# Attention and two MLPs on one core: the second pair's transposes and 46 unread products placed in front of the first scores, and a few tiles moved in on-chip memory

## The chip, the cores and the metric

The kernel runs on one core of one Trainium2 chip. The metric is device microseconds of one execution, smaller is better. The core has the engines TensorE (PE, with its weight loads shown as PEld), VectorE (DVE), ScalarE (ACT), GpSimd (POOL), and SyncE (SP), which here only issues DMAs.

## What is computed

Attention over 4 batches and 8 heads, 576 positions, head size 64, with a causal mask and a gate bias made from running sums of `max(s, 0)`; its output goes through a first MLP (512 to 1024 to 512, a softmax-weighted unit with a layer norm) and a second (512 to 2048 to 512). Cut to what matters:

```python
scores = scale * np.matmul(q, k.transpose(0, 1, 3, 2))
cum = np.cumsum(np.maximum(s, 0.0), axis=-1)
bias = -(cum[:, :, :, None] - cum[:, :, None, :])
scores = np.where(causal, -1000000000.0, scores + np.minimum(bias, 0.0))
attn = softmax(scores)
x = (attn @ v) as [2304, 512]
h = x @ w_in;  e = exp(h - max(h));  solu = h * e / (sum(e) + 1e-09)
x = layer_norm(solu) * g_ln @ w_out
h = x @ w2_in;  out = (h * np.clip(h + 3.0, 0.0, 6.0) / 6.0) @ w2_out
```

## The kernel before

Heads are worked in pairs (two heads of 64 rows side by side on 128 partitions). For a pair `p` of batch 0, `load_qk` (L396) loads q and k in natural order; `prep_whole` (L431 on) **turns** them: TensorE transposes six pieces of q and six of k against the identity matrix `ident` (L441), ACT scales q and DVE copies k out of PSUM (L446, L448). The bias is added by a second product: `gate_rows` makes running sums on DVE (L279 to L283), stores them as rows in DRAM (`rows_d`, L287), and `load_gates` (L428) brings four rows per head into the tiles `whole0` and `whole1`. `qk_whole` (L584) then makes the scores of a query tile `t` (128, 128, 128, 96, 96 rows): per head one product with the gate rows and one with q and k, in the same PSUM bank. Tiles 0 and 1 of all four pairs of batch 0 go first, later tiles afterwards. `tops` (L532, DVE) adds the mask and takes the row maxima, `exps` (L544, ACT) the exponentials, `norm_part` the reciprocals of the sums (L640, L641, DVE) and the scaling (L645, POOL); `tr` (L679) transposes the result, `av` (L708) multiplies by v.

The first MLP: `ffn1_x` splits a token tile in a high and a low part (`xh` on DVE L795, `xl` on POOL L799); `ffn1_h` (L813) is three products per piece with `w_in_h` and `w_in_l`; `ffn1_z` (L879) transposes, and `ffn1_out` (L900) multiplies `zh`, `zl` by `w_out_h`, `w_out_l`. The second MLP is L1072 and L1103. The weights come as 64-bit words and are decoded on ACT, DVE and POOL during the attention of batch 0.

The order of the work is not the order of the source. `Plan.add` records each step with its engine, an assumed duration, what it reads, writes and holds, and an assumed `lag` until a transfer has landed; `Plan.emit` runs a list scheduler over these numbers and writes every engine's instructions in the order that comes out. The numbers set the order alone: on the chip each instruction waits for the semaphores of what it truly needs. DMAs share eight semaphores in turn, so an issue also waits until the DMA that stands eight places ahead of it has landed.

Tiles are placed in the order in which the program asks for them. A tile pool on the right grows downward: `w_in_h`, `w_in_l`, `w_out` (chunks 0 to 4 of its 8), `g_sb`, then the working tiles `x`, `xh`, `xl`, `st`, `e`, `zh`, `zl`. Counted modulo 512 bytes, the tiles of the second MLP start at 480; in the first MLP `w_in_h` and `w_in_l` start at 448 and `xh`, `xl` at 320; `zh` and `zl` start at 448, `w_out` at 448 for chunks 0 to 4 and at 480 for chunks 5 to 7 (those lie in tiles of their own).

Of the kernel before, what the change touches and what calls it, by code (L numbers as in the profile page):

```python
# [10 lines left out]
F32 = mybir.dt.float32  # L11
# [29 lines left out]
CHUNKS = (3, 3, 4, 4, 4)  # L41
LAG = 2
DELAY = 3.5
X2_AT = 8
HOP_TO_PE, HOP_FROM_PE, HOP = 0.26, 0.2, 0.13

# [142 lines left out]
def kernel(ctx, tc, q, k, v, s, w_in, w_out, g_ln, w2_in, w2_out, out):  # L189
# [50 lines left out]
    def w_out_at(x, c):  # L240
        late = c >= KFF - LATE_OUT
        return w_out_t[x, late][:, c - (KFF - LATE_OUT) * late, :]

    w_out_part(False)
    g_sb = w1p.tile([P, KFF], F32, name="g_sb")


    at = ExitStack()
# [6 lines left out]
        return banks[plan.bank[key]]  # L255


    mask = ap1.tile([P, 480 + P], F32, name="mask")
    nc.gpsimd.memset(mask, 0.0)
    nc.gpsimd.affine_select(out=mask[:, 480:], in_=mask[:, 480:], pattern=[[-1, P]], compare_op=ALU.is_ge, fill=NEG, base=0, channel_multiplier=1)  # L260
# [5 lines left out]
    def gate_rows():  # L266


        s_sb = ap2.tile([P, S], F32, tag="y4", name="s_sb")[:NH]
        one = ap2.tile([P, S], F32, tag="y4", name="one")[:NH]  # L270
        cum = ap2.tile([P, NQ, 2, D], F32, tag="V", name="cum").rearrange("p c j d -> p (c j d)")[:NH, :S]
        pos = ap2.tile([P, PT_COLS], F32, tag="pt", name="pos", bufs=PT).bitcast(F32R)[:NH, : 2 * S]
        neg = ap2.tile([P, PT_COLS], F32, tag="pt", name="neg", bufs=PT).bitcast(F32R)[:NH, : 2 * S]

        def load():
            nc.sync.dma_start(out=s_sb, in_=s.rearrange("b h s -> (b h) s"))

        def sums():
            nc.vector.tensor_scalar_max(s_sb, s_sb, 0.0)  # L279
            nc.vector.tensor_tensor_scan(cum, one, s_sb, 0.0, ALU.mult, ALU.add)  # L280
            nc.vector.tensor_copy(pos[:, :S], cum)
            nc.vector.tensor_sub(pos[:, S:], cum, pos[:, :S].bitcast(F32))
            nc.vector.tensor_scalar_mul(neg, pos.bitcast(F32), -1.0)  # L283

        def put(i, r, src):
            dst = rows_d[:, i, r::2, :]
            nc.sync.dma_start(out=dst, in_=src)  # L287

        def zeros(j):
            whole_t[j] = ap1.tile([P, 4, S], F32, tag=f"stack{j}", name=f"whole{j}")  # L290
            nc.gpsimd.memset(whole_t[j][:, 2:4, :], 0.0)

        plan.add("SP", 0.45, load, writes=["s"], lag=2.0)
        plan.add("POOL", 2.2, lambda: nc.gpsimd.memset(one, 1.0), writes=["one"])
        plan.add("DVE", 3.0, sums, reads=["s", "one"], writes=["c"])
        ones = one.unsqueeze(1).to_broadcast([NH, 2, S])
        both = lambda c: c.bitcast(F32).rearrange("p (i s) -> p i s", i=2)
        for i, r, src, key in ((1, 0, both(pos), "c"), (0, 1, both(neg), "c"), (0, 0, ones, "one"), (1, 1, ones, "one")):
            plan.add("SP", 0.55, lambda i=i, r=r, src=src: put(i, r, src), reads=[key], writes=[f"rows/{i}{r}"], lag=2.0)
        for j in range(2):  # L300
            plan.add("POOL", 1.3, lambda j=j: zeros(j), writes=[f"zeros{j}"], new=[(f"stack{j}", 1, f"whole{j}")])

# [121 lines left out]
    def load_gates(p, a):  # L424
# [4 lines left out]

        plan.add("SP", 0.8, gates, reads=ROWS_D + [f"zeros{p % 2}", f"whole{p % 2}"], writes=[f"G{p}{a}"], new=[("G", 2, f"G{p}{a}")], lag=2.0)  # L430

    def prep_whole(p, name):

        n = S // 6
        i, raw_key, hl_key = "qk".index(name), f"raw{name}{p}", f"HL{p}"

        def turn(c0, key):
            if name == "q" and c0 == 0:
                hls[hl_key] = ap2.tile([P, 2, S], F32R, tag="HL", name=hl_key).bitcast(F32) if p < 2 else whole_t[p % 2][:, :2, :]
            for c in range(c0, c0 + 3):  # L440
                nc.tensor.transpose(bank(key)[:, (c - c0) * n : (c - c0 + 1) * n], raws[p, name][:n, c, :, :], ident[:n, :n])  # L441

        def put(c0, key):
            to = hls[hl_key][:, i, c0 * n : (c0 + 3) * n]
            if name == "q":
                nc.scalar.mul(to, bank(key)[:, : 3 * n], QK_SCALE)  # L446
            else:
                nc.vector.tensor_copy(to, bank(key)[:, : 3 * n])  # L448

        if name == "q":  # L450
            load_gates(p, 0)
        ring = [("HL0", 2, hl_key)] if p < 2 else []
        home = [] if p < 2 else [f"zeros{p % 2}", f"whole{p % 2}"]
        for c0 in (0, 3):
            key = f"pp{p}{name}{c0}"
            plan.add("PE", 3 * 0.083, lambda c0=c0, key=key: turn(c0, key), reads=[raw_key, *home], writes=[key],
                     new=ring if name == "q" and c0 == 0 else [], bank=key, after=[] if name == "q" and c0 == 0 else [f"pp{p}q0"])
            plan.add(*(("ACT", act(3 * n)) if name == "q" else ("DVE", dve(3 * n))), lambda c0=c0, key=key: put(c0, key), reads=[key, *home], writes=[f"{hl_key}/{name}{c0}"])
# [95 lines left out]
    def qk_whole(p, t):  # L554

        n, w = SZ[t], ST[t] + SZ[t]
        heads = (2 * p, 2 * p + 1)
        late = ST[t] >= CUT
        ts = [i for i in range(NQ) if (ST[i] >= CUT) == late]

        def homes():
            for h, x in zip(heads, "hl"):
                if p % 2 == 0:
                    ys[h, t] = ap2.tile([P, w], F32, tag=f"y{t}", name=f"y{h}_{t}")
                elif t == ts[0]:
                    cols = sum(ST[i] + SZ[i] for i in ts)
                    if late:
                        y = w1p.tile([P, LATE_OUT, DM], F32, tag=f"w_out_{x}1", name=f"yl{h}").rearrange("p c n -> p (c n)")
                    else:
                        y = ap2.tile([P, cols], F32, tag="y2", name=f"yf{h}")  # L570
                    o = 0
                    for i in ts:
                        ys[h, i] = y[:, o : o + ST[i] + SZ[i]]
                        o += ST[i] + SZ[i]

        def mm(c0, c1, keys):
            if c0 == 0:
                homes()
            for m in range(2):
                for j in range(2):  # L580
                    r = slice(j * D, (j + 1) * D)
                    g, hl = gates_at(p, j), hls[f"HL{p}"][r]
                    a, b = (hl[:, 0, :], hl[:, 1, :]) if m else (g[:, 0, :], g[:, 1, :])
                    nc.tensor.matmul(bank(keys[j])[:n, : c1 - c0], lhsT=a[:, ST[t] : w], rhs=b[:, c0:c1], start=(m == 0), stop=(m == 1))  # L584

        pieces = pieces_of(t)
        for c0, c1, at in pieces:
            keys = [f"sc{h}_{t}_{c0}" for h in heads]
            new = []
            if c0 == 0 and p % 2 == 0:  # L590
                new = [(f"y{t}", 2, f"y{h}_{t}") for h in heads]
            elif c0 == 0 and t == ts[0]:
                new = [("wlate", 1, f"yl{p}")] if late else [("y2", 2, f"yf{h}") for h in heads]
            plan.add("PE", 4 * max(0.07, 0.00033 * (c1 - c0)), lambda c0=c0, c1=c1, keys=keys: mm(c0, c1, keys),
                     reads=[f"HL{p}/{x}{c}" for x in "qk" for c in ((0, 3) if late else (0,))] + [f"G{p}{late:d}", f"whole{p % 2}"], writes=keys, new=new, bank=keys, after=[f"sc{heads[0]}_{t}_0"] if c0 else [])
            for h, key in zip(heads, keys):
                plan.add("DVE", dve(c1 - c0), lambda h=h, c0=c0, c1=c1, at=at, key=key: tops(h, t, c0, c1, at, key), reads=[key],
                         writes=[f"{y_key(h, t)}/{c0}", f"nmax{h}_{at}"])
        for h in heads:
            exps(h, t, pieces)  # L600
# [146 lines left out]
    def pairs(a):  # L747
# [3 lines left out]
        for p in range(NPAIR):  # L751
# [2 lines left out]
            turns = [] if last is None else [(0.4, lambda h=h, gi=gi: tr(h, gi)) for gi in ((1, 2, 3) if last[1] else (0,)) for h in (2 * last[0], 2 * last[0] + 1)]  # L754
            extra = []
            if not a:
                if p + 1 < NPAIR:
                    extra = [(0.3, lambda p=p: prep_qk(p + 1, "q")), (0.3, lambda p=p: prep_qk(p + 1, "k"))]
                extra += [(0.0, lambda p=p: load_qk(p + 2))] if p + 2 <= NPAIR else []
                extra += [(0.0, lambda p=p: load_v(p + 1, 0))] if p + 1 < NPAIR else [(0.0, lambda: load_v(0)), (0.0, lambda: load_gates(0, 1))]  # L760
# [44 lines left out]
    def ffn1_h(i, f, kk):  # L805
        key = f"h{i}_{f}"

        def mm():
            if f == kk == 0:
                sts[i] = bcp.tile([P, 16], F32, tag="st", name=f"st{i}")  # L810
                es[i] = bcp.tile([P, 2, 512], F32, tag="e", name=f"e{i}")
            for m in range(3):
                nc.tensor.matmul(bank(key), lhsT=xs[i][m // 2][:, kk, :], rhs=(w_in_l if m == 1 else w_in_h)[:, kk, f * 512 : (f + 1) * 512],  # L813
                                 start=(kk == 0 and m == 0), stop=(kk == KDM - 1 and m == 2))
# [161 lines left out]
    for name in "qk":  # L976
        prep_qk(0, name)
    load_qk(1)
    load_v(0, 0)
    plan.add("SP", 0.5, lambda: nc.sync.dma_start(out=g_sb, in_=g_ln.rearrange("(c p) -> p c", p=P)), writes=["g"], lag=2.0, after=["HL0/k0"])  # L980
    for b, share in enumerate(SHARES):
# [212 lines left out]
```

## Time and profile before

| | us |
|---|---|
| median of 3 runs | 842.57 (842.36 to 842.8) |
| profiled execution, its own time | 840.6 |
| its span | 838.8 |
| PE busy | 810.9 (97%) |
| DVE busy | 438.5 (52%) |
| ACT busy | 399.4 (48%) |
| POOL busy | 209.9 (25%) |

The span runs from the first to the last instruction of the profiled execution; 1.8 us of its time lie outside. A busy PE is an engine with a matmul in flight, whatever its clock. The column PEclk of a table by stretches gives the TensorE clock that was granted, 1.00 being 2.4 GHz and 0.50 being 1.2 GHz. The chain of waits is followed back from the last instruction: each step is what released the next one.

### The profile page before, as it was taken

What the parts mean: (1) busy time and instruction counts of PE and PEld (TensorE: products, weight loads), DVE (VectorE), ACT (ScalarE), POOL (GpSimd) and SP (SyncE); (2) the same over time, 40 slices, a digit from 0 to 9 for tenths busy, and PEclk for the clock granted to TensorE, in tenths of its full rate; (3) what the DMA queues carried; (4) which work ended last, traced back from release to release, by engine and by line L of the source; (5) the groups of instructions that cost most, each with busy time, mean ns of one, the idle gap of its engine ahead of it and who ended that gap; (6) DMA issues with size and microseconds to landing.
All of it is one profiled execution on the core that took longest, in us unless ns stands there. A gap on an engine that the chain in (4) does not pass through costs nothing.

```text
span 838.8 us, 13546 instructions
## 1 busy us (share of the span) xinstructions
PE 810.9 (97%) x4864; PEld 686.1 (82%) x4864; DVE 438.5 (52%) x1125; ACT 399.4 (48%) x928; POOL 209.9 (25%) x309
## 2 busy tenths in 40 slices
PE   3889999999999999999999999999999999999997
PEld 2555688898898889888999999998888888888886
DVE  3787887746855674739826992233222232222221
ACT  2575767755765575736635762244222322232222
POOL 2564644424632364327412220000000000000000
PEclk9999999999999999999999999999999999999999
DMA  6753596855656465323615640012000300010001
GB/s 163 194 150 112 126 214 148 175 121 125 130 119 137 99 130 121 65 95 117 198 38 192 215 152 1 0 63 89 1 0 1 101 1 0 1 51 1 0 1 50
DMA packets 95938, 77.52 MB, mean 92 GB/s; under 512 B 64288, under 2 KB 78112, under 8 KB 95872
## 3 DMA queue, kind: packets, MB, share of 16 engines
q1 hardware_dynamic: 93568, 68.27, 32.7%
q10 hardware_dynamic: 2304, 8.39, 3.0%
q8 instruction: 38, 0.62, 0.3%
q14 instruction: 28, 0.23, 0.1%
HBM read 45.38 MB, written 10.03 MB: 66 GB/s over the span
## 4 chain that ended last, share of the span: by engine, by line
PE 91%; DVE 4%; POOL 2%; DMA 2%; issue 1%; ACT 1%; POOLq 0%; DVEq 0%; SPq 0%; ACTq 0%
PE bank L1072 24%; PE bank L1103 23%; PE bank L900 11%; PE bank L813 10%; PE bank L708 6%; PE bank L679 5%; PE bank L611 5%; PE bank L584 3%; PE bank L879 2%; PE bank L474 1%; POOL y L645 1%; DVE y L532 1%; DMA stack<-HL12k 1%; DMA rows_d<-neg 1%; POOL y L627 0%
## 5 line engine op out<-in xcount | busy, mean ns | idle before, releaser
L1072 PE MATMUL bank<-x2h,w 128*128 128x512 f32 (+1 forms) x640 | 183.7, 368 | 0.0
L1103 PE MATMUL bank<-w,gh 128*128 128x512 f32 x576 | 177.0, 390 | 0.0
L1080 DVE SCALAR_TENSOR_TENSOR g<-g,bank 128x512 f32<-128x512 f32 (+1 forms) x80 | 50.7, 633 | 204.4 <-ACT g L1076 204.1
L1072 PEld LDWEIGHTS bank<-x2h,w 128*128 128x128 f32 x640 | 118.8, 188 | 17.5
L1076 ACT ACTIVATE g<-bank 128x512 f32<-128x512 f32 (+1 forms) x80 | 44.5, 556 | 178.2 <-PE bank L1072 177.9
L1103 PEld LDWEIGHTS bank<-w,gh 128*128 128x128 f32 x576 | 107.7, 188 | 21.0
L1072 PE MATMUL bank<-x2l,w 128*128 128x512 f32 (+1 forms) x320 | 117.8, 368 | 0.0
L1103 PE MATMUL bank<-w,gl 128*128 128x512 f32 x288 | 111.8, 391 | 0.0
L532 DVE CUSTOM_DVE_ANT_0 y<-bank,mask 96x288 f32<-96x288 f32 (+4 forms) x168 | 74.7, 467 | 57.4 <-PE bank L611 38.0
L544 ACT ACTIVATE y<-y,nmax 128x256 f32<-128x256 f32 (+4 forms) x140 | 83.4, 598 | 39.8 <-DVE nmax L532 27.5
L627 POOL TENSOR_SCALAR y<-y,rsum 128x128 f32<-128x128 f32 (+4 forms) x120 | 68.6, 590 | 103.8 <-DVE rsum L623 45.2
L900 PE MATMUL bank<-zh,w_out_h 128*128 128x256 f32 x288 | 82.8, 287 | 0.0
L900 PE MATMUL bank<-zl,w_out_h 128*128 128x256 f32 x288 | 81.2, 282 | 0.0
L900 PE MATMUL bank<-zh,w_out_l 128*128 128x256 f32 x288 | 81.2, 282 | 0.0
L1088 DVE TENSOR_TENSOR gl<-g,gh 128x512 fp32r<-128x512 f32 (+1 forms) x80 | 51.8, 647 | 42.2 <-ACT gh L1084 41.9
L1084 ACT CAST gh<-g 128x512 fp32r<-128x512 f32 (+1 forms) x80 | 46.2, 578 | 47.4 <-DVE g L1080 47.3
L1072 PEld LDWEIGHTS bank<-x2l,w 128*128 128x128 f32 x320 | 60.1, 188 | 7.5
L1103 PEld LDWEIGHTS bank<-w,gl 128*128 128x128 f32 x288 | 54.0, 188 | 11.3
L813 PE MATMUL bank<-w_in_h,xh 128*128 128x512 f32 x144 | 60.9, 423 | 0.8 <-DVE xh L795 0.8
L611 PE MATMUL bank<-stack 128*96 128x288 f32 (+4 forms) x288 | 57.8, 317 | 0.8 <-DMA stack<-HL12k 0.8
L813 PE MATMUL bank<-w_in_h,xl 128*128 128x512 f32 x144 | 56.9, 395 | 0.6 <-POOL xl L799 0.6
L813 PE MATMUL bank<-w_in_l,xh 128*128 128x512 f32 x144 | 56.8, 394 | 0.0
(220 smaller groups left out, 1356.4 us busy)
## 6 DMA issues: line engine op xcount, KB each, us to landing
raw_w2i<-in_moe_w_in_dram SPq DMA_DIRECT2D x16, 512.0 KB
raw_w2o<-in_moe_w_out_dram SPq DMA_DIRECT2D x16, 512.0 KB
rawq<-in_q_dram SPq DMA_DIRECT2D x32, 144.0 KB
rawk<-in_k_dram SPq DMA_DIRECT2D x32, 144.0 KB
x_d<-x2s SPq DMA_DIRECT2D x36, 128.0 KB
out_dram<-ob SPq DMA_DIRECT2D x18, 256.0 KB
raw_wi<-in_moe_w_in_dram ACTq DMA_DIRECT2D x8, 512.0 KB
raw_wo<-in_moe_w_out_dram ACTq DMA_DIRECT2D x8, 512.0 KB
```

What stands on the lines that cost most here:

```text
L532: nc.vector.tensor_tensor_reduce(out=ys[h, t][:n, c0:c1], in0=bank(key)[:n, : c1 - c0], in1=mask[:n, 480 + n - w + c0 : 480 + n - w + c1], ...
L544: nc.scalar.activation(out=y[:n], in_=y[:n], func=AF.Exp, bias=nmax[:n, h, t : t + 1], scale=-1.0, accum_out=sums[:n, h, t : t + 1])
L611: nc.tensor.matmul(bank(key)[:n, : c1 - c0], lhsT=ss[:, 2 - 2 * m, ST[t] : w], rhs=ss[:, 3 - 2 * m, c0:c1], start=(m == 0), stop=(m == 1))
L627: nc.gpsimd.tensor_scalar(ys[h, t][:n], ys[h, t][:n], rsum[:n, h, t : t + 1], 1.0, ALU.mult, ALU.mult)
L708: nc.tensor.matmul(bank(key)[j * D : (j + 1) * D, lo - c0 : c1 - c0], lhsT=vs[v_key(p, a)][:n, jj, j, :], rhs=pts[pt_key(2 * p + j, a)][:n ...
L813: nc.tensor.matmul(bank(key), lhsT=xs[i][m // 2][:, kk, :], rhs=(w_in_l if m == 1 else w_in_h)[:, kk, f * 512 : (f + 1) * 512], start=(kk ...
L900: nc.tensor.matmul(bank(key)[:, : 2 * P], lhsT=w_out_at(w, kk)[:, m * P : (m + 1) * P], rhs=z[:, kk, :], start=(kk == 0 and i == 0), stop= ...
L1072: nc.tensor.matmul(bank(key)[:, :w], lhsT=wt[:, a, 0, c * P : (c + 1) * P], rhs=x[:, c, :w], start=(c == 0 and i == 0), stop=(c == KDM - 1 ...
L1080: nc.vector.scalar_tensor_tensor(out=gg, in0=gg, scalar=6.0, in1=bank(key)[:, :w], op0=ALU.min, op1=ALU.mult)
L1084: nc.scalar.copy(gh[:, :w], gg[:, :w])
L1088: nc.vector.tensor_sub(gl[:, :w], gg[:, :w], gh[:, :w].bitcast(F32))
L1103: nc.tensor.matmul(bank(key), lhsT=g_t[ci, m][1 + i // 2][:, t * P : (t + 1) * P], rhs=w2[m][:, i % 2, 1, :], start=(m == 0 and i == 0), s ...
```

## The change

Four edits. In `pairs` and in the main body the turns of pair 1 are no longer spread over the first steps but planned right after pair 0's, and the first scores of pair 0 must wait until pair 1's last turn has begun (`after=["pp1k3"]`); the gate rows' stores are planned with a lag of 4.5 in place of 2.0. A new helper `keep_clock` issues bf16 products of `ident` with itself (128x256) into the bank that the next step overwrites; nothing reads them: 26 ahead of pair 1's q turn, 10 ahead of its k turn, 10 ahead of the first scores. `g_sb` is placed ahead of `w_out` and `st` grows from 16 to 64 numbers (two buffers), so `xh` and `xl` now start at 448 modulo 512 as `w_in` does, and `w_out` starts at 480 for all eight chunks while `zh`, `zl` stay at 448. A tile of 32 numbers, `apart_too`, moves all attention tiles by 128 bytes; `ident` stays.

```diff
+FILL = dict(q=26, k=10, s=10)
...
+    g_sb = w1p.tile([P, KFF], F32, name="g_sb")
     w_out_part(False)
-    g_sb = w1p.tile([P, KFF], F32, name="g_sb")
...
+    ap1.tile([P, 32], F32, name="apart_too")
     mask = ap1.tile([P, 480 + P], F32, name="mask")
...
-            plan.add("SP", 0.55, lambda i=i, r=r, src=src: put(i, r, src), reads=[key], writes=[f"rows/{i}{r}"], lag=2.0)
+            plan.add("SP", 0.55, lambda i=i, r=r, src=src: put(i, r, src), reads=[key], writes=[f"rows/{i}{r}"], lag=4.5)
...
+    def keep_clock(n, key):
+
+        x = ident.bitcast(BF16)
+        for _ in range(n):
+            nc.tensor.matmul(bank(key)[:, : 2 * P], lhsT=x[:, :P], rhs=x, start=True, stop=True)
...
+            if p == 1 and c0 == 0:
+                keep_clock(FILL[name], key)
...
+            if p == t == c0 == 0:
+                keep_clock(FILL["s"], keys[0])
...
-... after=[f"sc{heads[0]}_{t}_0"] if c0 else [])
+... after=[f"sc{heads[0]}_{t}_0"] if c0 else ["pp1k3"] if p == 0 and not late else [])
...
-                if p + 1 < NPAIR:
+                if 0 < p < NPAIR - 1:
                     extra = [(0.3, lambda p=p: prep_qk(p + 1, "q")), (0.3, lambda p=p: prep_qk(p + 1, "k"))]
...
-                sts[i] = bcp.tile([P, 16], F32, tag="st", name=f"st{i}")
+                sts[i] = bcp.tile([P, 64], F32, tag="st", name=f"st{i}")
...
     load_qk(1)
+    for name in "qk":
+        prep_qk(1, name)
     load_v(0, 0)
```

The start of TensorE's order, before: the turns of pair 0 (`rawq_120`, `rawk_123`), then scores of pair 0 (`whole_126` holds its gate rows) mixed with the turns of pair 1 (`rawq_148`, `rawk_163`).

```order
L441 MATMUL bank_100<-ident,rawk_123 128x96 x3
L584 MATMUL bank_101<-whole_126 128x128
L584 MATMUL bank_102<-HL_138 128x128
L441 MATMUL bank_103<-ident,rawq_148 128x96 x3
L584 MATMUL bank_97<-whole_126 128x256
L584 MATMUL bank_98<-HL_138 128x256
L441 MATMUL bank_99<-ident,rawk_163 128x96 x3
L584 MATMUL bank_103<-whole_135 128x128
L584 MATMUL bank_102<-HL_183 128x256
L441 MATMUL bank_99<-ident,rawq_198 128x96 x3
L679 MATMUL bank_97<-ident,y_0_177 128x128
```

The same place now (L438 is the unread product, L451 the turn, L596 the score, L691 the transpose of `y`; pair 1 is `rawq_149`, `rawk_164`, pair 2 `rawq_229`, `rawk_257`; 26, 10 and 10 pairs of L438 rows stand at the three places).

```order
L451 MATMUL bank_100<-ident,rawk_124 128x96 x3
L438 LDWEIGHTS ident
L438 MATMUL bank_101<-ident 128x256
L451 MATMUL bank_101<-ident,rawq_149 128x96 x3
L451 MATMUL bank_103<-ident,rawk_164 128x96 x3
L596 MATMUL bank_97<-whole_127 128x128
L596 MATMUL bank_100<-HL_139 128x256
L596 MATMUL bank_101<-whole_136 128x128
L596 MATMUL bank_104<-HL_178 128x256
L451 MATMUL bank_97<-ident,rawq_229 128x96 x3
L451 MATMUL bank_100<-ident,rawk_257 128x96 x3
L691 MATMUL bank_101<-ident,y_0_241 128x128
```

Both turns of pair 1 have moved ahead of all scores, the scores of pairs 0 and 1 stand in one block, and pair 2's k turn has moved ahead of the first transposes of `y`.

SP's order at the gate rows, before and now (`whole_126`/`whole_127` for pair 0, `whole_135`/`whole_136` for pair 1; `V0a` is v of pair 0, and the issue shown brings 128x2x64 numbers, 64 KB).

```order
L396 DMA rawk_163<-in_k_dram 96x6x64 [waits DMAHW6_49]
L428 DMA whole_126<-rows_d 4x2x576 [waits DMAHW2_49,DMAHW7_49,DMAHW1_49,Pool_49]
L414 DMA V0a<-in_v_dram 128x2x64
L980 DMA g_sb<-in_moe_g_ln_dram 128x8x1
L428 DMA whole_135<-rows_d 4x2x576 [waits DMAHW3_49,Pool_49]
```

```order
L398 DMA rawk_164<-in_k_dram 96x6x64 [waits DMAHW6_49]
L416 DMA V0a<-in_v_dram 128x2x64 [waits DMAHW7_49]
L994 DMA g_sb<-in_moe_g_ln_dram 128x8x1 [waits DMAHW0_49]
L430 DMA whole_127<-rows_d 4x2x576 [waits DMAHW2_49,DMAHW1_49,Pool_49]
L430 DMA whole_136<-rows_d 4x2x576 [waits DMAHW4_49,Pool_49]
```

The loads of `V0a` and of `g_sb` (1024 single numbers) have moved ahead of the gate rows of pair 0.

## Rows read from the trace of the kernel before

**Rows 1.** The page, part 1: busy time of each engine.

```profile
PE 810.9 (97%) x4864; PEld 686.1 (82%) x4864; DVE 438.5 (52%) x1125; ACT 399.4 (48%) x928; POOL 209.9 (25%) x309
```

**Rows 2.** Chain of waits, 0 to 62 us: start us, us, what.

```profile
8.61 4.26 DMA rows_d<-neg
13.02 2.40 DMA whole<-rows_d
```

**Rows 3.** By stretches: length, busy us (instructions) of each engine, PEclk, DMA share, GB/s.

```profile
7.40:15.50 8.10, 0.00 (x0) 0.00 (x0) 3.00 (x6) 0.67 (x1) 0.00 (x0) 1.00 0.97 246
15.56:17.03 1.47, 1.47 (x8) 1.25 (x9) 0.12 (x1) 0.00 (x0) 0.00 (x0) 1.00 0.39 27
17.03:18.18 1.15, 1.15 (x7) 0.93 (x7) 0.41 (x4) 0.37 (x1) 0.00 (x0) 1.00 0.00 0
18.18:20.19 2.01, 2.01 (x9) 1.19 (x9) 0.00 (x0) 1.22 (x6) 0.00 (x0) 1.00 0.34 82
...
21.26:22.85 1.59, 1.58 (x17) 1.13 (x16) 1.59 (x8) 0.31 (x1) 0.60 (x1) 1.00 1.13 276
22.85:27.76 4.91, 2.43 (x19) 1.74 (x19) 3.55 (x15) 4.17 (x17) 4.14 (x6) 1.00 0.82 155
27.80:31.30 3.50, 3.50 (x21) 2.47 (x22) 1.87 (x11) 1.86 (x6) 1.92 (x5) 0.52 0.68 205
```

**Rows 4.** TensorE in order of time: start us, us, line, operation, tiles, shape.

```profile
18.18 1.23 PE L584 MATMUL bank<-whole 64*128 64x256 f32 x4
...
21.81 0.60 PE L584 MATMUL bank<-whole 64*128 64x256 f32 x4
```

**Rows 5.** SP's DMA issues in order of time, same columns.

```profile
10.21 1.74 SPq L396 DMA_DIRECT2D rawk<-in_k_dram  x2
...
14.13 0.46 SPq L980 DMA_DIRECT2D g_sb<-in_moe_g_ln_dram  x1
```

**Rows 6.** By stretches, the microsecond after the `g_sb` load was issued.

```profile
15.00:16.00 1.00, 0.44 (x3) 0.47 (x4) 0.00 (x0) 0.00 (x0) 0.00 (x0) 1.00 0.63 26
```

**Rows 7.** All engines in order of time: POOL scales pair 0's first tiles.

```profile
24.29 2.55 POOL L645 TENSOR_SCALAR y<-y,rsum 128x128 f32<-128x128 f32 x4 [0.77 <-DVE rsum L641]
```

**Rows 8.** Chain of waits: from those tiles' transposes to pair 2's first scores.

```profile
27.33 0.50 PE bank L441 x6
27.83 2.90 PE bank L584 x16
```

**Rows 9.** TensorE in order of time: inside an unbroken run of L813.

```profile
410.09 0.40 PE L813 MATMUL bank<-w_in_h,xh 128*128 128x512 f32 x1
...
414.74 0.40 PE L813 MATMUL bank<-w_in_h,xl 128*128 128x512 f32 x1
```

**Rows 10.** TensorE in order of time: L1103 just after a change of shape, and later.

```profile
500.24 0.63 PE L1103 MATMUL bank<-w,gh 128*128 128x512 f32 x2
...
502.32 0.51 PE L1072 MATMUL bank<-x2h,w 128*128 128x384 f32 x2
...
553.92 1.52 PE L1103 MATMUL bank<-w,gh 128*128 128x512 f32 x6
555.28 0.84 PE L1103 MATMUL bank<-w,gl 128*128 128x512 f32 x3
```

**Rows 11.** TensorE in order of time: L900, chunks 5 to 7, then chunks 0 to 4.

```profile
426.80 0.28 PE L900 MATMUL bank<-zh,w_out_h 128*128 128x256 f32 x1
...
427.74 0.28 PE L900 MATMUL bank<-zl,w_out_h 128*128 128x256 f32 x1
...
431.79 0.28 PE L900 MATMUL bank<-zh,w_out_h 128*128 128x256 f32 x1
...
433.57 0.28 PE L900 MATMUL bank<-zh,w_out_h 128*128 128x256 f32 x1
```

**Rows 12.** Chain of waits: ahead of the stretch that TensorE fills.

```profile
55.23 1.48 POOL w_in_l L348
56.70 4.22 POOL y L645 x5
```

More of the change, by code (lines that the diff above doesn't have):

```diff
@@ L594, in qk_whole @@
             plan.add("PE", 4 * max(0.07, 0.00033 * (c1 - c0)), lambda c0=c0, c1=c1, keys=keys: mm(c0, c1, keys),
-                     reads=[f"HL{p}/{x}{c}" for x in "qk" for c in ((0, 3) if late else (0,))] + [f"G{p}{late:d}", f"whole{p % 2}"], writes=keys, new=new, bank=keys, after=[f"sc{heads[0]}_{t}_0"] if c0 else [])
+                     reads=[f"HL{p}/{x}{c}" for x in "qk" for c in ((0, 3) if late else (0,))] + [f"G{p}{late:d}", f"whole{p % 2}"], writes=keys, new=new, bank=keys, after=[f"sc{heads[0]}_{t}_0"] if c0 else ["pp1k3"] if p == 0 and not late else [])
             for h, key in zip(heads, keys):
```

## The prediction

> **What bounds the kernel now.** I read the busy times first: TensorE is busy for 810.9 us of the span [rows 1], so time can be won only where it waits, where its clock is low, or in the products themselves. The stretches then show where it waits: between 7.4 and 15.5 it does nothing at all [rows 3], the longest pause of the span. The chain of waits says for what: the `neg` rows' store, issued at 8.61, takes 4.26, and the gate rows' load after it 2.40 [rows 2], so the first scores begin at 15.56. What follows runs slowly. Four 64x256 products take 1.23 us at 18.18 and 0.60 at 21.81 [rows 4]; one set of six turns takes 1.15 at 17.03 and 0.50 at 27.33 [rows 3, 8]. That is half speed, 1.2 in place of 2.4 GHz, although the column of the granted clock says 1.00 there; I go by durations until the column shows a change of its own, the fall to 0.52 after 27.8 [rows 3]. So TensorE starts cold after a long pause, and warms up while the first pairs' scores wait for it. The profiled execution took 840.6, 2.0 below the median of the runs (842.57); I make the sum against 840.6 and carry the difference over to the median.
>
> **When the first scores can start now.** Call that moment S; it was 15.56. Three things must be over.
>
> The gate rows: their load still cannot be issued before 12.87 (8.61 + 4.26), but the data now stand behind `V0a` and `g_sb`. 64 KB at 246 GB/s is 0.3 us; the single numbers of `g_sb` kept the DMA engines 0.63 busy for a microsecond that moved 26 GB/s [rows 6], so 0.6 to 0.8. The rows land 1.1 later, at about 16.5. If nothing else were late, S would be 16.6: the early end.
>
> Pair 1's k: its two loads are issued from 10.21 to 11.95 [rows 5]. How long they take to land no row says. The nearest is the `neg` store in the same crowded stretch, 4.26 from issue; the gate load's 2.40 is the other end [rows 2]. That gives 14.4 to 16.2. I take 16.2, as the DMA engines are 0.97 busy until 15.5 [rows 3]. By the same row q, issued ahead of 10.21, is there at about 14.5.
>
> The unread products: no bf16 product stands in the trace. The nearest row in shape is L900, 128x256, which starts every 0.12 us (fifteen from 431.79 to 433.57) [rows 11]; at the low clock I double it to 0.24. The first 26 begin at 7.4 and end between 10.5 (all fast) and 13.6 (all slow), before q lands either way: free. Then q's turns 14.5 to 15.0, ten products to 16.2, k's turns 16.2 to 16.7 and the last ten to 17.9, all at the high clock. **S is about 17.9**, set by k's load and the last ten products, not by the gate rows.
>
> **From S to pair 2's scores.** The scores of one pair at the high clock take 1.59 (21.26 to 22.85) [rows 3], so both are done at S + 3.2. POOL started its scaling at 24.29 [rows 7], 1.44 after the last of these scores, behind the row maxima, exponentials and sums; I keep 1.44, as VectorE's order again puts pair 0's sums behind pair 1's maxima. From POOL's start to the last transpose of `y` it is 3.04 (24.29 to 27.33) [rows 7, 8]. Pair 2's k turn, 0.50 behind those transposes before [rows 8], now stands ahead of them, where TensorE waits for POOL: free. So pair 2's scores begin at S + 7.7 = 25.6, against 27.83. **The start gives 2.2 us.** The ends: 3.5 for S = 16.6; minus 1.5 for the slow clock (below).
>
> **The clock fall at 27.8.** From 22.85 to 27.76 TensorE was busy for 2.43 us, all of it turns and transposes, and then the clock fell to 0.52 for 3.5 us [rows 3]. The new order again has only turns and transposes between pair 1's scores and pair 2's, for about 4.5 us, so I expect the fall again and put down nothing for it. The Trainium skill (TensorE: Matmul & The Clock Gate, Part 4: PE-mode transpose) says that transposes do not count as PE work for the clock; the trace agrees. By it, moving turns forward would warm nothing and only the unread products do. If transposes did count, the denser order would avoid the fall and the sum would be about 1.3 us better.
>
> **The first MLP's offsets.** L813 now has both operands at 448, as L1072 and L1103 have at 480. Inside a run L813 starts every 0.2325 us (20 starts, 410.09 to 414.74) [rows 9]. L1103, equal all along, starts every 0.227 late in a run (six in 1.36 us from 553.92), but its first nine after a change of shape take 2.08, 0.231 each (500.24 to 502.32) [rows 10]. Of the 432 products of L813, 267 stand in runs of three or six, so most never get past nine; some 90 do. 90 times 0.005 is 0.5 us. The ends: nothing, and 432 times 0.0055 = 2.4. L900 goes the other way: chunks 0 to 4 lose their equal offsets. But chunks 5 to 7, unequal before, start every 0.1175 (426.80 to 427.74, eight starts) and chunks 0 to 4 every 0.1187 [rows 11]; 540 products by 0.0012 are 0.6 us better if that is the offset, and 0.6 worse if unequal is what costs. I take 0.2 better. The 128 bytes of `apart_too` move both operands of a score alike; only transposes against `ident` see another distance. By the same 0.0012 on 624 of them that is 0.7 either way, and I take 0.
>
> **The rest of the order.** The scheduler's new numbers shift many rows behind the start. The work is the same, and after 61 us TensorE has hardly a pause, so a lead there is kept to the end. I take 0 for it with 1.5 either way. Sum: 2.2 + 0.5 + 0.2 = 2.9 less; 840.6 becomes 837.7, and the median 842.57 becomes **839.7**.
>
> **The rivals.** *The lead is lost on the way* (0.22). Up to 61 us the chain goes through POOL: `w_in_l` 1.48, then five scalings 4.22 [rows 12]. If the weights' decoding, not the pairs, paces that, TensorE waits there as long as before, and only 0.7 for the offsets is left: 841.9. For it: POOL, DVE and ACT feed those steps in turn. Against it: each scaling there belongs to a pair, and pairs come earlier.
>
> *The clock falls again before the unread products have done their work* (0.15), the case on the other side. Between the first 26 and q's turns TensorE pauses for 1 to 4 us, and the turns themselves may not hold the clock (the 22.85 stretch [rows 3]). If it is low at 14.5, turns take 1.15 and ten products 2.4: 14.5 + 1.15 + 2.4 = 18.05, k's turns to 19.2, ten more to 21.6. With S = 21.6 pair 2's scores begin at 29.3, 1.5 later than before; with 0.7 from the offsets the total is 843.4, 844.1 without them, and 846.6 if the scores stay slow as well (3.2 more). It decides from S = 20.1 (27.83 less 7.7) on: beyond that the products cost more than the cold clock did.
>
> *The offsets carry it* (0.10): equal offsets bring every L813 to 0.227, 2.4 in place of 0.5: 837.8.
>
> *It does not do what it says* (0.03): the order shows the moved turns and the products, but L900's operands end up less alike than before; with 0.6 lost there and nothing won in L813, 841.0.
>
> **How the numbers follow.** My forecast, S near 17.9 and the lead kept, has 0.50 and reaches from 838.2 to 841.2. The range is 836.8 to 843.8: down to the offsets' case with S = 16.6, up to the slow-clock case, with 1.5 of reordering inside. Two runs of this kernel can be told apart from about 0.2%, 1.7 us. Faster than 840.9: most of the forecast (0.43), the offsets' case and a little of the lost lead, 0.57. Slower than 844.2 or so: slow clock in its bad half, plus reordering that hurts, 0.15. Same: 0.28.
>
> **What would show it.** Right: unread products 0.12 us apart at the latest from q's turns on; turns of pair 1 in 0.5 us; first scores between 17 and 18.5, each pair's in 1.6; pair 2's first scores near 25.6; L813 near 0.232 in short runs. Wrong: products 0.24 apart ahead of the first scores (slow clock), first scores on time but TensorE filled only from 61 us again (lead lost), or L813 at 0.227 from the first product of a run (offsets).

## The result: slower by 1.3%

The changed kernel takes 852.6 us, the median of 4 runs (851.54 to 854.76), against 842.47 for the kernel before, run beside it on the same chip (4 runs, 842.16 to 842.8). The ratio is 1.0127, with a 95% interval from 1.0113 to 1.0140. The forecast was 839.7, in a range from 836.8 to 843.8: wrong in sign, and the result lies outside the range.

Page of the changed kernel, its span, part 1, and the granted clock of part 2:

```profile
span 849.8 us, 13657 instructions
PE 821.2 (97%) x4910; PEld 694.6 (82%) x4910; DVE 438.4 (52%) x1125; ACT 399.9 (47%) x928; POOL 207.1 (24%) x309
PEclk9999989999999999999999999999999999999999
```

TensorE is busy for 821.2 us in place of 810.9 [rows 1], of which some 7.4 are the 46 unread products (3.69, 2.11 and 1.64 in the rows below). Without them it does useful work for 813.8, which is 2.9 more than before, and does none for 36.0 (849.8 less 813.8), which is 8.1 more than before (838.8 less 810.9 is 27.9). So most of the 11.0 us by which the span grew are **new pauses**, and the rest is the same work done at a lower clock: the mean granted clock is 0.987 against 0.997.

The start. TensorE in order of time, from its first turns to the first scores (start us, us, engine, line, operation, tiles; L451 are turns, L438 the unread products, L596 the scores):

```profile
6.71 0.53 PE L451 MATMUL bank<-ident,rawk 96*128 96x96 f32 x2
7.03 3.69 PE L438 MATMUL bank<-ident 128*128 128x256 bf16 x26
14.50 0.69 PE L451 MATMUL bank<-ident,rawq 96*128 96x96 f32 x6 [3.78 <-DMA rawq<-in_q_dram]
15.02 2.11 PE L438 MATMUL bank<-ident 128*128 128x256 bf16 x10
16.92 1.17 PE L451 MATMUL bank<-ident,rawk 96*128 96x96 f32 x6
17.88 1.64 PE L438 MATMUL bank<-ident 128*128 128x256 bf16 x10
19.46 0.49 PE L596 MATMUL bank<-whole 64*128 64x128 f32 x4
```

The first 26 products are over at 10.7, and TensorE waits for q's load until 14.50, as long as forecast. The ten products behind q's turns then take 2.11 and k's turns 1.17, against 0.69 for q's: half speed, and by the trace's clock records the clock is at 0.5 from 15.3 to 18.7. The first scores begin at 19.46 (15.56 before, 17.9 forecast).

What followed. Chain of waits of the changed kernel, 0 to 62 us (start us, us, what):

```profile
26.85 2.53 PE bank L596 x16
...
31.09 1.88 DMA whole<-rows_d
...
38.97 2.83 DMA whole<-rows_d
```

Pair 2's scores begin at 26.85 where they began at 27.83 [rows 8]: 1.0 earlier, not 2.2. Behind them the chain runs twice through loads of gate rows, which it did not do before once the first scores had begun. TensorE's waits from 10 to 130 us, changed kernel, then before (line waited for: us in total, times, longest us):

```profile
PE bank L623 <- DMA stack<-HL5k: 5.4, 1, 5.4
PE bank L451 <- DMA rawq<-in_q_dram: 3.8, 1, 3.8
PE bank L596 <- DMA whole<-rows_d: 3.4, 2, 1.8
```

```profile
PE bank L584 <- DMA whole<-rows_d: 8.2, 1, 8.2
```

The longest new wait stands far from the edit, at 114 us: L623, the late scores, waits 5.4 us for a stack load of the sixth pair (tile `HL5k`). By stretches around it (length, busy us and instructions of each engine, granted clock, DMA share, GB/s), changed kernel, then before:

```profile
105.00:114.30 9.30, 9.26 (x77) 7.00 (x74) 9.27 (x26) 7.91 (x21) 3.42 (x5) 1.00 0.79 186
114.30:120.00 5.70, 0.26 (x2) 0.28 (x2) 4.20 (x14) 1.89 (x5) 3.50 (x6) 0.79 1.02 272
120.00:125.00 5.00, 5.00 (x21) 4.42 (x21) 0.00 (x0) 0.00 (x0) 0.00 (x0) 0.55 0.55 114
```

```profile
114.00:125.00 11.00, 10.37 (x67) 8.70 (x65) 8.97 (x27) 6.70 (x18) 6.94 (x9) 1.00 1.05 255
```

The pause takes 5.4 us, and then TensorE works for five more at a clock of 0.55. How the loss grows can be followed by single products: the first of the first MLP (L813, now L825) begins at 58.84 instead of 53.96 (4.9 later), the 61st at 127.96 instead of 117.95 (10.0 later), the last of L900 (now L912) at 455.21 instead of 444.12 (11.1 later), and from there on nothing is added.

Why the stack load comes late stands in SyncE's issues in order of time (changed kernel, 103 to 116 us; the second number is the time from this issue's start to its end, its waits in between included):

```profile
103.79 1.58 SPq L398 DMA_DIRECT2D rawq<-in_q_dram  x2
...
107.85 5.35 SPq L398 DMA_DIRECT2D rawk<-in_k_dram  x2
113.30 0.47 SPq L502 DMA_DIRECT2D stack<-HL5k  x1
113.86 0.62 SPq L503 DMA_DIRECT2D stack<-HL5k  x1
```

The two issues for the seventh pair's keys (`rawk`) take 5.35 us, where the two for its queries take 1.58. SyncE's waits from 105 to 125 us name what held them:

```profile
SPq L398 <- DMA raw_wo<-in_moe_w_out_dram: 3.3, 1, 3.3
```

That is a 512 KB block of weights, issued by ScalarE at 106.14. Its completion is counted on the same semaphore as the keys' second load (both records in the trace name it), so SyncE issues this load only when the block is in, at 112.9. The data of `HL5k` had been packed by 109.02, but their load stands behind. In the kernel before, the same keys' loads were issued at 102.92 and 103.28, beside this block (102.94), and none of them waited for it.

That is one part of the pause. The other is when TensorE asks. Changed kernel (chain, then TensorE in order of time), and below it the kernel before (SyncE and TensorE in order of time):

```profile
113.86 5.80 DMA stack<-HL5k
119.75 0.77 PE L623 MATMUL bank<-stack 128*96 128x288 f32 x2 [5.45 <-DMA stack<-HL5k]
```

```profile
111.96 0.80 SPq L493 DMA_DIRECT2D stack<-HL5k  x1
118.65 0.69 PE L611 MATMUL bank<-stack 128*128 128x384 f32 x4
```

In the kernel before, this load landed at 118.06 by the trace's completion records, only 1.6 us ahead of the changed kernel's 119.66. TensorE did not wait there, because its own order had other products and transposes for it until 118.65. In the changed order it runs out of them at 114.3. So, next to the kernel before, the later load makes some 1.6 of the 5.4 us, and the rest is that TensorE comes to these scores some 4 us sooner.

The Trainium skill (DMA: Bandwidth & Descriptors, Anatomy of one DMA) says that a DMA's wait for a semaphore takes place on the issuing engine's sequencer, before dispatch; the trace agrees, with 3.3 us of SyncE's wait for a transfer which ScalarE had issued.

### The profile page after: what moved, and what is told of

The parts are those of the page before. It is cut to its first block, busy times and chain, and to the rows that moved or that the text cites. A ratio compares the mean times of both kernels' runs of the same rounds, so it can differ in the third digit from the quotient of the medians.

```text
span 849.8 us, 13657 instructions
## 1 busy us (share of the span) xinstructions
PE 821.2 (97%) x4910; PEld 694.6 (82%) x4910; DVE 438.4 (52%) x1125; ACT 399.9 (47%) x928; POOL 207.1 (24%) x309
## 4 chain that ended last, share of the span: by engine, by line
PE 88%; DVE 4%; DMA 3%; POOL 2%; issue 1%; ACT 1%; SPq 0%; POOLq 0%; ACTq 0%; DVEq 0%
PE bank L1086 23%; PE bank L1117 23%; PE bank L912 12%; PE bank L825 10%; PE bank L691 5%; PE bank L720 5%; PE bank L623 5%; PE bank L596 2%; PE bank L891 2%; PE bank L484 1%; POOL y L657 1%; DMA stack<-HL5k 1%; DMA stack<-HL12k 1%; DMA rawq<-in_q_dram 1%; DMA whole<-rows_d 1%
## 5 line engine op out<-in xcount | busy, mean ns | idle before, releaser
L554 ACT ACTIVATE y<-y,nmax 128x128 f32<-128x128 f32 (+4 forms) x140 | 83.4, 597 | 34.0 <-DVE nmax L542 27.5
L639 POOL TENSOR_SCALAR y<-y,rsum 128x128 f32<-128x128 f32 (+4 forms) x120 | 67.7, 582 | 117.7 <-DVE rsum L635 66.3
L912 PE MATMUL bank<-zh,w_out_h 128*128 128x256 f32 x288 | 83.1, 288 | 0.0
L912 PE MATMUL bank<-zh,w_out_l 128*128 128x256 f32 x288 | 81.3, 282 | 0.0
L912 PE MATMUL bank<-zl,w_out_h 128*128 128x256 f32 x288 | 81.3, 282 | 0.0
L1102 DVE TENSOR_TENSOR gl<-g,gh 128x512 fp32r<-128x512 f32 (+1 forms) x80 | 53.8, 672 | 42.2 <-ACT gh L1098 41.8
L623 PE MATMUL bank<-stack 128*96 128x288 f32 (+4 forms) x288 | 58.4, 318 | 6.7 <-DMA stack<-HL5k 5.4
L825 PE MATMUL bank<-w_in_h,xh 128*128 128x512 f32 x144 | 61.0, 424 | 0.0
L691 PE MATMUL bank<-ident,y 128*128 128x128 f32 (+2 forms) x420 | 53.7, 264 | 3.9 <-POOL y L657 2.6
L825 PE MATMUL bank<-w_in_l,xh 128*128 128x512 f32 x144 | 57.3, 398 | 0.0
```

The lines of the kernel that those rows point to most:

```text
L554: nc.scalar.activation(out=y[:n], in_=y[:n], func=AF.Exp, bias=nmax[:n, h, t : t + 1], scale=-1.0, accum_out=sums[:n, h, t : t + 1])
L623: nc.tensor.matmul(bank(key)[:n, : c1 - c0], lhsT=ss[:, 2 - 2 * m, ST[t] : w], rhs=ss[:, 3 - 2 * m, c0:c1], start=(m == 0), stop=(m == 1))
L639: nc.gpsimd.tensor_scalar(ys[h, t][:n], ys[h, t][:n], rsum[:n, h, t : t + 1], 1.0, ALU.mult, ALU.mult)
L691: nc.tensor.transpose(bank(key)[: SZ[jj], c : c + SZ[t]], ys[h, t][: SZ[t], ST[jj] : ST[jj] + SZ[jj]], ident[: SZ[t], : SZ[t]])
L912: nc.tensor.matmul(bank(key)[:, : 2 * P], lhsT=w_out_at(w, kk)[:, m * P : (m + 1) * P], rhs=z[:, kk, :], start=(kk == 0 and i == 0), stop= ...
L1102: nc.vector.tensor_sub(gl[:, :w], gg[:, :w], gh[:, :w].bitcast(F32))
```

## The experiments

Theory 1: the planner's new numbers put SyncE's loads in an order in which some stand behind a weight block; TensorE pauses for them, and each pause is followed by a stretch at the lower clock. Theory 2: the unread products and the early turns cost the time. Theory 3: the offsets cost it. Each run is compared with runs of the kernel before beside it (842.07 to 842.24 us in the median, four groups).

**Run 1, the offsets alone.** `g_sb` ahead of `w_out_part`, `apart_too`, `st` of 64, on the kernel before.

> The kernel before with nothing but the offsets of the change (g_sb ahead of w_out, the operands apart, st of 64). Theory 1 (the new numbers of the planner put SyncE's gate-row loads behind a weight load, TensorE pauses for them, and each pause is followed by a stretch at the lower clock): the offsets are innocent, 839.5 to 842.5 us against 842.5 before. Theory 2 (the early turns and the unread products at half clock start the loss): the same. Theory 3 (the offsets cost the time): 850 or more.

840.74 us, ratio 0.9982 (0.9971 to 0.9992): 1.5 us faster. Theory 3 falls. In the trace the mean distance between two starts in a row, those over 0.3 us left out, fell by 1.7 ns for L813 (233.4 to 231.7) and by 0.5 for L900 (121.1 to 120.6); the second MLP's products kept theirs (206.5 and 228.0). Times 432 and 864 that is 0.7 and 0.4 us of the 1.5.

**Run 2, the change without its products.**

```diff
-FILL = dict(q=26, k=10, s=10)
+FILL = dict(q=0, k=0, s=0)
```

> The change with none of its 46 unread products, all else in the same order, which leaves out only work that nobody reads. Theory 1: the later order is still that of the change, so 849 to 855 us. Theory 2: the loss goes with the products, 840 to 845 us. Theory 3: as the change, 851 to 854 us.

851.94 us, ratio 1.0112 (1.0093 to 1.0131), as the change itself within the intervals. The products neither cause the loss nor save anything; theory 2 falls as far as it rests on them.

**Run 3, the old order with the early turns and the products.** The order of the kernel before, permuted as it is emitted:

```diff
+        for x in "qk":
+            for c in (0, 3):
+                early += self.writers[f"pp1{x}{c}"] + self.writers[f"HL1/{x}{c}"]
+        first = self.writers["sc0_0_0"][0]
...
+        for i in order[:at] + early + order[at:]:
```

> The order of the kernel before, kept row for row, with only the second pair's four turns and the 46 unread products put ahead of the first scores, and no offsets. Theory 1: without the planner's new order behind it the loss is gone, 839 to 844 us, and of the five falls of the clock that the change shows at most two are left. Theory 2: the loss stays, 849 to 855 us. Theory 3: no offsets here, 840 to 843 us; it can only be told from theory 1 by the first run.

845.42 us (839.37 to 847.63 in 12 runs), ratio 1.0027 (1.0007 to 1.0047). This kept theory 1's main point, some two thirds of the loss being gone with the new order, but not its size: the moved turns or the products cost something in the old order too (runs 6 and 8 part them), and four falls of the clock were left, not two.

**Run 4, the gate rows' lag back at 2.0.**

```diff
-            plan.add("SP", 0.55, ..., writes=[f"rows/{i}{r}"], lag=4.5)
+            plan.add("SP", 0.55, ..., writes=[f"rows/{i}{r}"], lag=2.0)
```

> The change with the planner's lag for the gate rows back at the kernel before's 2.0, which puts both pairs' gate rows on SyncE's queue ahead of V and of the weights. Theory 1: SyncE's wait for the weight load ahead of the second gate rows (5.5 us) goes, and with it at least the pauses of TensorE at 31 and 40 us and the falls of the clock behind them: 842 to 848 us. Theory 2: as the change, 850 to 855 us. Theory 3: as the change.

851.81 us, ratio 1.0105 (1.0087 to 1.0124): a miss for theory 1 as I had put it, with the gate rows as its main case. TensorE's waits from 10 to 130 us in this run say why:

```profile
PE bank L623 <- DMA stack<-HL5q: 7.8, 1, 7.8
...
PE bank L596 <- DMA whole<-rows_d: 2.3, 2, 2.0
```

The gate rows' 3.4 us became 2.3, while the stack load's 5.4 became 7.8. So the next run went for the stack load.

**Run 5, the stack loads ahead.** The change, with two loads of SyncE moved behind the sixth pair's stack loads:

```diff
+        late = [*self.writers["V4/1"], *self.writers["rawk6"]]
+        order = [i for i in order if i not in late]
+        at = order.index(self.writers["S5_1/g"][0]) + 1
+        for i in order[:at] + late + order[at:]:
```

> The change, with two loads of SyncE (half of the values of the fifth pair, the keys of the seventh) put behind the two stack loads that the sixth pair's scores at 114 us wait for. In the change the keys' load holds the queue from 109.6 to 112.9 us, until the transfer of a weight block (raw_wo) whose completion semaphore it reuses is in, and TensorE waits 5.4 us and runs at half clock behind it. Theory 1 (SyncE's new order): that wait goes, with one or two of the falls at 117 to 124 us: 844 to 848 us. Rival (the later order is late as a whole, and another wait takes the place of this one, or TensorE's banks): 850 to 854 us.

846.9 us (846.15 to 847.92 in five executions, one more took 1004.95), ratio 1.0062 (1.0048 to 1.0075): 5.7 us of the change's 10.1 are won back by the place of two loads, 3.6 if the two profiled executions are compared (851.54 and 847.92). SyncE's issue, TensorE's first scores from it and the stretches of this run:

```profile
110.27 0.46 SPq L506 DMA_DIRECT2D stack<-HL5k  x1
117.95 0.48 PE L627 MATMUL bank<-stack 128*96 128x288 f32 x2 [1.72 <-DVE t_wo L334]
```

```profile
114.30:120.00 5.70, 3.98 (x29) 3.61 (x28) 5.51 (x19) 3.84 (x10) 4.65 (x6) 1.00 0.73 193
120.00:125.00 5.00, 5.00 (x34) 4.36 (x33) 3.03 (x10) 3.22 (x9) 0.35 (x2) 1.00 1.20 210
```

The stack load is issued 3 us earlier, TensorE is busy for 3.98 of the 5.70 us in place of 0.26, and the clock stays at 1.00. The rival, another wait in its place, falls for the most part. A pause of 1.72 us is left at the same scores, although the second stack load landed at 117.70, ahead of the kernel before's 118.06; that TensorE comes early to these scores was not tried apart.

**Runs 6 and 7, the old order with the turns alone, without and with the offsets.** Run 3 with `FILL` at 0, then with the three edits of run 1 as well.

> The kernel before's order, with only the second pair's four turns ahead of the first scores: no products, no offsets. Theory 1 (the turns are worth what their place in the wait saves; the old order behind them keeps it): 840 to 841.5 us against 842.1. Rival (the lead is lost on the way, as each later load comes when it came): 841.8 to 842.5. Rival (the third run's extra 2.4 us come from the moved turns and not from the products): 843.5 to 846.

844.42 us, ratio 1.0028 (1.0009 to 1.0046).

> The run before this one with the change's offsets: if the gains of the turns and of the offsets (1.5 us) add up, 838.5 to 840 us; if the offsets' gain needs the order of before untouched, 840 to 842.

842.05 us (839.66 to 844.53 in 12 runs), ratio 1.0001 (0.9986 to 1.0015). Run 6 misses theory 1 and lies where its second rival put it, and the gains do not add up in run 7: the early turns, which start pair 2's scores 1.5 us sooner in run 6's trace (26.26 against 27.76), end 2.3 us slower without the offsets and 1.3 to 1.6 slower than the offsets alone (840.74, ratio 0.9982). SyncE and TensorE in order of time in run 6:

```profile
26.36 3.99 SPq L406 DMA_DIRECT2D rawk<-in_k_dram  x2
30.45 0.73 SPq L438 DMA_DIRECT2D whole<-rows_d  x2
```

```profile
32.97 1.01 PE L604 MATMUL bank<-whole 64*96 64x480 f32 x2 [1.94 <-DMA whole<-rows_d]
35.58 1.08 PE L604 MATMUL bank<-whole 64*96 64x480 f32 x1 [1.59 <-DMA whole<-rows_d]
```

It is the same thing in a second place. The keys of the fourth pair wait for a weight block (`raw_wi`, 3.3 us by SyncE's waits), and behind them stand the gate rows of pair 0's late half. In the kernel before, those rows were issued at 29.87 and TensorE did not wait for them. Now they are issued at 30.45 and TensorE, ahead of its old times, waits twice, 3.5 us in all, after which the clock stands at 0.66 from 35 to 40.

**Run 8, the products alone,** all 46 ahead of the first scores of the kernel before:

```diff
+FILL = dict(s=46)
```

> The kernel before with the 46 unread products ahead of its first scores, in the 8 us in which TensorE waits, and nothing moved. Theory A (the products cost the third run its 2.4 us and more, because the clock rises on them, TensorE waits again, and the clock falls under the first scores): 843 to 847 us, with a fall at 14 to 22 us. Theory B (they are done by 13 us in a wait that is there anyway, and cost and give nothing): 841.5 to 842.7. Theory C (they keep the clock up, as meant): 839.5 to 841.5.

842.46 us, ratio 1.0008 (0.9999 to 1.0017): B, with A's mechanism in the trace. The stretches of this run:

```profile
10.00:13.00 3.00, 3.00 (x30) 2.69 (x28) 1.12 (x2) 0.68 (x1) 0.00 (x0) 1.00 1.02 316
13.00:16.00 3.00, 0.78 (x9) 0.49 (x6) 0.00 (x0) 0.00 (x0) 0.00 (x0) 1.00 0.88 140
16.00:24.00 8.00, 7.92 (x44) 5.79 (x44) 3.67 (x19) 3.16 (x13) 1.27 (x1) 0.57 0.71 150
```

Between 10 and 13 us the products are twice as dense as at the start, TensorE waits again, and the first scores run at 0.57. Here the lower clock is nearly free. In the kernel before these scores ran at half speed as well, until 21 us [rows 4], and TensorE waits behind them for POOL in any case [rows 7, 8]; which of the two makes it free was not tried apart.

**Run 9, the gate rows ahead.** Run 7, with the late gate rows put ahead of two other loads:

```diff
+        late = [*self.writers["V1a/1"], *self.writers["rawk3"]]
+        order = [i for i in order if i not in late]
+        at = order.index(self.writers["G01"][0]) + 1
+        for i in order[:at] + late + order[at:]:
```

> The seventh run (old order, the turns moved, offsets), with the late gate rows of the first pair put ahead of two other loads on SyncE's queue, the keys of the fourth pair and half of the second pair's values. In the seventh run the keys' load holds the queue from 26.4 to 29.5 us behind a weight block (raw_wi), so that the gate rows land at 32.4 and TensorE waits from 30.5. If this wait is what eats the turns' lead: 837.5 to 839.5 us, and the runs lie closer together than the seventh run's 839.7 to 844.5. Rival (the lead only runs into the next thing): 840.5 to 842.5.

**838.18 us** (837.62 to 840.38), ratio 0.9949 (0.9936 to 0.9962): faster than the kernel before by 4.1 us, and than the changed one by some 14. SyncE and TensorE of this run, from 27 us:

```profile
27.50 0.60 SPq L443 DMA_DIRECT2D whole<-rows_d  x2
28.15 0.39 SPq L429 DMA_DIRECT2D V1a<-in_v_dram  x1
28.60 1.26 SPq L411 DMA_DIRECT2D rawk<-in_k_dram  x2
```

```profile
29.76 0.66 PE L464 MATMUL bank<-ident,rawq 96*128 96x96 f32 x6
30.35 1.05 PE L609 MATMUL bank<-whole 64*96 64x480 f32 x4
```

The gate rows leave 3 us sooner than in run 6, and the scores follow the turns without a wait. By single products the lead is 2.3 us at pair 2's scores (25.46), 1.2 at the first product of the first MLP (52.76) and 2.1 at the last of L900 (442.07): this time, the offsets included, it reaches the end. The profiled execution has no fall of the clock at all once it has risen at 21.8 us.

**Run 10, both loads ahead in the change;** run 5 with run 9's move, `rawk3` alone. **Run 11,** the same without the products.

> The fifth run with the gate rows at 31 us put ahead of the fourth pair's keys too, so that both loads that TensorE waited for in the change are mended and all else of it is kept, its 46 unread products too. If the two waits are the whole loss of the change: 840 to 843.5 us. Rival (a third place, as the pause at 64 us, carries some 3 us): 843.5 to 846. Rival (nothing, as the gate rows land no earlier): 846 to 847.5.

843.48 us (839.22 to 847.7 in 12 runs), ratio 1.0011 (0.9993 to 1.0028).

> The tenth run without the 46 unread products (work that nobody reads). If they neither give nor cost: within 1 us of the tenth run. If they keep the clock up once nothing waits behind them: 1.5 to 3 us slower than the tenth run. If their half-clock end at 15 to 19 us is what is left of the loss: 1.5 to 3 us faster than it.

843.92 us, ratio 1.0013 (0.9999 to 1.0027). With the two loads mended, 9.1 of the change's 10.1 us are gone, still without touching its products, its turns or the rest of its order. What is left to the offsets alone (840.74) is some 2.7 us. TensorE's waits of run 10 from 24 to 130 us, in the slowest of its twelve executions (847.7), name where it may stand, and they were not tried one by one:

```profile
PE bank L604 <- DMA whole<-rows_d: 2.8, 2, 2.5
PE bank L492 <- DMA rawk<-in_k_dram: 2.1, 1, 2.1
PE bank L459 <- DMA rawk<-in_k_dram: 2.0, 1, 2.0
```

Again loads. Only the 2.1 us of L492, at 125 us, are for one that was put behind (the seventh pair's keys); the 2.0 us are for the third pair's keys and the 2.8 for gate rows. The trace of run 11 is of its fastest execution (839.2) and has waits of 2.1 us for those keys and 1.6 for gate rows, and none at 125 us. The products stay worth nothing.

**Run 12, the gate rows ahead without the turns:** the kernel before with run 1's offsets and run 9's move.

> The ninth run without the moved turns: the kernel before's order and the offsets, with only the two loads of SyncE put behind the late gate rows. If the ninth run's gain over the first (838.2 against 840.7 us) belongs to the turns, which need these gate rows early to keep their lead: 840 to 841.5 us, as the first run. If it belongs to the gate rows alone: 837.5 to 839.5.

843.23 us, ratio 1.0009 (1.0000 to 1.0018): 2.3 us slower than the offsets alone, which neither case had. So run 9's gain does not belong to the gate rows alone. SyncE in order of time in this run, and TensorE's wait:

```profile
29.42 0.60 SPq L433 DMA_DIRECT2D whole<-rows_d  x2
32.88 0.39 SPq L419 DMA_DIRECT2D V1a<-in_v_dram  x1
33.33 1.00 SPq L401 DMA_DIRECT2D rawk<-in_k_dram  x2
```

```profile
PE bank L446 <- DMA rawk<-in_k_dram: 3.4, 1, 3.4
```

Without the early turns TensorE frees the gate rows' place later (SyncE waits up to 3.7 us for the scores there), the two loads behind them meet the next weight block, and the keys' turns wait 3.4 us. The same two moves are worth 2.6 us together (840.74 to 838.18, ratios 0.9982 and 0.9949), and each of them alone costs 1.3 to 2.5.

## Why the prediction was wrong

**The step that failed** is "The rest of the order": "The work is the same, and after 61 us TensorE has hardly a pause, so a lead there is kept to the end. I take 0 for it with 1.5 either way." By the sum of the prediction it measured some 12.6: the time rose by 10.1, while the start gave 1.0 at pair 2's scores and the offsets 1.5. About 9 of it is the place of a few loads in SyncE's order: two behind the stack loads are worth 5.7 us (run 5), and one keys' load behind the gate rows another 3.4 (run 10). The other 3.5 stay open. The step took the few pauses for a property of the work, when they come out of the queues' orders against each other. At 114 us the new numbers put the stack loads behind a keys' load that waits for a weight block, and they also bring TensorE to the scores 4 us sooner; what the second costs alone was not tried. The prediction went through SyncE's order only up to the first scores, and through TensorE's only up to pair 2's.

**The start** was right in its mechanism and missed in size. q's load came at 14.36 (I had 14.5), k's was not what was late, the gate rows were not either, and the last ten products did set the first scores. But S was 19.5 and not 17.9, since the products and k's turns ran at half speed from 15 us on: the condition of the rival on the slow clock, which I had given 0.15. Its S of 21.6 and its price were not met, though: the products at half clock cost nothing in the total (runs 2, 8, 11). From S to pair 2's scores it took 7.4 where I had 7.7, and the start gave 1.0 in place of 2.2.

**The rival "the lead is lost on the way"** is what became of the turns, by another mechanism than its own. I had POOL and the decoding in mind, with TensorE waiting "as long as before". In run 6 the lead runs into gate rows that leave no earlier than before, and since a slow stretch follows the pauses there, more is lost than the lead was (844.42).

**The clock at 27.8** fell at about the place expected (0.57 from 25 to 29 us). The forecast had no place for the other falls, from 15.3, 42.6, 66.5 and 117.7 us. Each follows a pause; the one ahead of 66.5 (1.3 and 0.3 us) was for DVE and POOL and not for a load of SyncE. Avoiding the fall at 27.8 would be worth 1.7 us by the prediction's own rows (3.5 us at 0.52), not 1.3. The 1.00 that the column shows during the slow start is no grant: the clock records of the kernel before begin only at 21.1 us, and the column reads 1.00 ahead of the first. In run 9 the same stretch is denser, busy for 3.03 of 4.70 us from 21.9 to 26.6 with four score products among the turns, and no fall follows it. That is in the direction of "if transposes did count", but the score products stand in it too, so it decides nothing about the Trainium skill's rule (TensorE: Matmul & The Clock Gate, Part 4: PE-mode transpose).

**The offsets** were right: 0.7 expected, 1.5 measured (0.7 to 2.4), with gains in both L813 and L900 as taken (0.7 and 0.4 by the trace, for 0.5 and 0.2). That the offsets are equal cannot be what helps in both: L813's became equal and those of L900's chunks 0 to 4 unequal, and both gained. The lower end of the range, the offsets' case with S = 16.6, comes to 836.5 by its own terms and not to 836.8.

## What to carry to other kernels

Where a planner sets the order, compare the queues' orders over the whole stretch that it plans, and look on the issuing queue for a load that someone waits for behind a load that can itself be held by a large transfer: putting two loads behind the ones that were waited for was worth 5.7 us here, where the edit at the start could give 2.2 by its own reckoning. Compare with it when the waiting engine asks: the same load was nearly as late in the kernel before, and cost nothing there. A start that comes earlier is worth something only if the loads that the next pauses depend on come earlier as well (run 7 against run 9); try both together, since each alone can cost. Filling a wait with unread products so as to keep the clock up was worth nothing in three comparisons.

## What the runs showed of the hardware

A DMA issue can be held by a transfer of another engine's queue. SyncE waited for blocks of 512 KB that ScalarE had issued for 1.8, 5.2, 3.9 and 3.3 us in the changed kernel, for 3.3 in run 6, 3.1 in run 7 and 3.9 in run 9, with loads of 18 to 288 KB behind. Of the 5.2 us, 1.4 passed before ScalarE had issued the block. Such a wait costs only what someone waits for behind it: in run 9, TensorE's longest wait for a load after 20 us is 0.4 us.

The clock does not follow the program alone. Run 3's twelve executions took from 839.37 us at a mean granted clock of 0.997 to 847.6 at 0.989; run 9's six stayed within 2.8 us at 0.993 to 1.000. Runs 3, 6, 7, 10 and 11 spread over 5 to 8.5 us each, runs 1, 8, 9 and 12 over 2.3 to 2.8. What sets whether a given pause is followed by a fall was not settled: behind the 1.72 us of run 5 there is none, behind the 1.76 us at 41.9 us of the changed kernel there is one.
